# The experts of a mixture layer in three phases of 768 tokens with Strassen products of 384 columns, in place of two phases of 1152 with 288

## The chip, the core and the metric

One core of one Trainium2 chip runs the whole program. The metric is the time of one execution on the device, in microseconds (us), as the median of several runs. The core has five engines that work side by side, each with its own queue that it works off in order: TensorE (PE in the rows) for matmuls, VectorE (DVE), ScalarE (ACT) and GpSimd (POOL) for elementwise work, SyncE (SP) for issuing transfers. Engines wait for each other by semaphores.

## What is computed

```python
N, D, E, F = (2304, 512, 8, 1024)

def _moe2_ref(x, w_gate, w1, w2):
    logits = x @ w_gate
    logits = logits - logits.max()
    P = np.exp(logits)
    for _ in range(8):
        P /= P.sum(1, keepdims=True) + 1e-09
        P /= P.sum(0, keepdims=True) + 1e-09
        P *= N / E
    out = np.zeros((N, D), dtype=np.float32)
    for e in range(E):
        h = np.maximum(x @ w1[e], 0.0)
        ye = h @ w2[e]
        out += P[:, e:e + 1] * ye
    return out

def reference(attn, moe, moe2):
    a = _attn_ref(**attn)                 # 4 batches, 8 heads, 576 positions, causal with decay
    x = tokens_first(a)                   # (2304, 512)
    x = _moe_ref(x, **moe)                # gated SiLU layer, width 1536
    return _moe2_ref(x, **moe2)           # the experts
```

Every token goes through every expert; the gate only weighs the eight results, after eight rounds of normalising its rows and columns ("balancing" below).

## The kernel before

Attention and the gated layer come first (until about 710 us) and are the same in both kernels, up to their last unit, `moe_unit(3)`, into which the first loads of the experts are merged. What follows is the expert stage.

**Slices.** An expert's hidden width of 1024 is worked off in four slices of 256. The tokens are worked off in phases, since the sum over experts, `acc`, is kept on chip for the tokens of one phase only: two phases of 1152 tokens, so 2 x 8 x 4 = 64 slices. For each slice `wload(i)` fetches a piece of `w1` and of `w2` (512 KB each) and splits every number into a rounded part and a rest, because a product in full precision is made of three matmuls of rounded operands (hi x hi, hi x lo, lo x hi). The sums that Strassen's scheme needs of `w1` (tile `sm`) are made by DVE (L544), the rounded parts by ACT (L550, L554), the rests by POOL (L142: tiles `w1l`, `w2l`).

**Up.** `eup(i, g)` computes relu(x w1) for one slice and for one group `g` of 576 tokens, with seven Strassen products in place of eight, each of 288 token columns and six matmuls (L578, `pa`, 128x288). DVE combines the products (L587: tiles `u`, `c`), ACT takes one copy and the relu (L598, L592: `ah`), DVE the rest of the relu (L593: `al`). The products are written to five PSUM buffers in turn.

**Down.** `edown` multiplies with the slice of `w2`: six matmuls of 512 columns for each tile of 128 tokens (L150, `py`), written to two PSUM buffers in turn; DVE adds them to `acc`, weighed by the balanced gate `lg` (L630; the first expert, unweighed, at L623; ACT scales that sum later, at L626). A slice of 1152 tokens has 84 product matmuls and 54 of 512 columns.

**Operands of x.** The seven token-side operands of the Strassen products, in rounded parts and rests, make up `xf`. `xload(b)` makes them for 576 tokens: it reads x back from memory (`xst`), DVE makes four sums (L508: `xt`), ACT the rounded parts (L512: `xf<-xst`, `xf<-xt`), POOL the rests (L142, the same names). There is one buffer for each group, so those of the second phase are made at the turn of the phases, around 1474 to 1518 us.

**Balancing.** After the first slice `gate()` and `balance()` make `lg`: eight rounds, each of nine small DVE instructions (L665 to L679) with one small matmul in the middle of it (L674, `pz`, which sums over partitions). Each round needs the one before it.

**Order.** The order in which each engine works off these instructions is set at build time: a scheduler plays the program through and gives each engine's queue its order; the code's order is only its starting point. The queues then run as they are.

## Time and profile before

| | |
|---|---|
| time, median of 3 runs | 2275.65 us (2272.15 to 2277.56) |
| profiled execution, its own time | 2276.13 us |
| its span, first to last instruction | 2274.3 us |
| PE busy | 2224.4 us, 98% of the span |
| DVE busy | 1688.4 us, 74% |
| POOL busy | 884.6 us, 39% |
| ACT busy | 849.7 us, 37% |
| mean granted clock of TensorE | 0.995 of full speed |

The span is 1.8 us shorter than the time of that same execution. A row of the profile names the line of the code, the engine, the operation, the tile written and the tiles read. Matmuls overlap in PE's pipeline, so that the duration of one (0.3 us) is longer than the distance between two starts; the distance is what a matmul costs.

### The profile page before, as it was taken

Reading aid. Unit: us, or ns where it says so; the run is one execution under the profiler, and the core shown is the slowest. Engines: PE = TensorE matmul, PEld = TensorE weight load, DVE = VectorE, ACT = ScalarE, POOL = GpSimd, SP = SyncE. Lnnn points to the kernel's source line nnn. Section 1 sums busy time; section 2 is a strip of 40 time slices with the busy share of each in tenths; the row PEclk is TensorE's granted clock in tenths of the full one; section 3 lists DMA queues with packets and bytes.
Section 4 is the critical chain, followed back from the end, with each engine's and each line's share of the span. In section 5 each row is a group of like instructions: output and inputs, shape, how many; then the busy total and the mean of one; then the engine's idle time right before and its main releaser. Section 6 shows DMA issues by size and latency. Waiting matters only on the chain.

```text
span 2274.3 us, 36164 instructions
## 1 busy us (share of the span) xinstructions
PE 2224.4 (98%) x13881; PEld 2019.3 (89%) x13881; DVE 1688.4 (74%) x3385; ACT 849.7 (37%) x1936; POOL 884.6 (39%) x668
## 2 busy tenths in 40 slices
PE   7899999999999999999999999989999999999999
PEld 5698899999999898988988989979889898898897
DVE  6678854544535798888878888886888787887876
ACT  7766754454322433322323222333232232322321
POOL 6869863342423432323323233353233232332320
PEclk9999999999999999999999999999999999999999
DMA  8666664454644211111111111121111111111101
GB/s 246 196 213 217 214 229 159 163 171 148 232 160 153 70 46 40 47 47 38 56 38 47 47 39 56 48 90 51 43 43 51 38 56 38 47 47 38 56 29 51
DMA packets 95469, 215.97 MB, mean 95 GB/s; under 512 B 10000, under 2 KB 52288, under 8 KB 83264
## 3 DMA queue, kind: packets, MB, share of 16 engines
q1 hardware_dynamic: 95296, 213.66, 29.1%
q8 instruction: 109, 1.79, 0.3%
q14 instruction: 64, 0.52, 0.1%
HBM read 185.02 MB, written 28.61 MB: 94 GB/s over the span
## 4 chain that ended last, share of the span: by engine, by line
PE 85%; DVE 6%; DMA 4%; ACT 2%; issue 1%; POOL 1%; SPq 0%; DVEq 0%; ACTq 0%; POOLq 0%
PE py L150 39%; PE pa L578 29%; PE pm L150 11%; DMA st<-wf 2%; PE ps_o L340 2%; PE ps_t L309 1%; DVE al L593 1%; DMA xst<-xd 1%; PE ps_s L272 1%; PE ps_s L268 1%; DVE np L274 1%; DVE xt L508 1%; PE ps_o L332 1%; DVE c L587 0%; DMA qk<-qkT 0%
## 5 line engine op out<-in xcount | busy, mean ns | idle before, releaser
L578 PE MATMUL pa<-xf,w1h 128*128 128x288 f32 x3584 | 749.2, 295 | 7.0 <-DVE c L587 6.6
L578 PEld LDWEIGHTS pa<-xf,w1h 128*128 128x128 f32 x3584 | 597.7, 188 | 45.9 <-DVE c L587 8.4
L630 DVE SCALAR_TENSOR_TENSOR acc<-py,lg,acc 128x512 f32<-128x512 f32 x531 | 395.1, 744 | 241.2 <-PE py L150 240.9
L578 PE MATMUL pa<-xf,w1l 128*128 128x288 f32 x1792 | 527.4, 295 | 0.0
L142 POOL TENSOR_TENSOR w2l<-w,w2h 128x1024 fp32r<-128x1024 f32 x64 | 154.8, 2420 | 825.2 <-ACT w2h L554 825.0
L150 PE MATMUL py<-w2h,ah 128*128 128x512 f32 x1152 | 454.1, 394 | 4.2 <-DVE acc L623 2.5
L150 PE MATMUL py<-w2l,ah 128*128 128x512 f32 x1152 | 454.1, 394 | 0.0
L150 PE MATMUL py<-w2h,al 128*128 128x512 f32 x1152 | 453.2, 393 | 0.0
L593 DVE SCALAR_TENSOR_TENSOR al<-c,ah 128x288 fp32r<-128x288 f32 x512 | 426.7, 860 | 7.4 <-ACT ah L592 6.7
L592 ACT ACTIVATE ah<-c 128x288 fp32r<-128x288 f32 x512 | 208.1, 443 | 590.9 <-PE py L150 318.9
L578 PEld LDWEIGHTS pa<-xf,w1l 128*128 128x128 f32 x1792 | 337.0, 188 | 10.5
L150 PE MATMUL pm<-xh,w 128*128 128x288 f32 x1536 | 326.5, 298 | 3.4 <-DVE xa L431 1.9
L150 PEld LDWEIGHTS py<-w2h,al 128*128 128x128 f32 x1152 | 216.3, 188 | 49.9
L150 PEld LDWEIGHTS pm<-xh,w 128*128 128x128 f32 x1536 | 252.0, 188 | 6.2 <-DVE xa L431 2.5
L150 PEld LDWEIGHTS py<-w2h,ah 128*128 128x128 f32 x1152 | 216.4, 188 | 33.3 <-DVE acc L623 2.9
L150 PEld LDWEIGHTS py<-w2l,ah 128*128 128x128 f32 x1152 | 216.3, 188 | 26.0
L142 POOL TENSOR_TENSOR w1l<-w,w1h 128x256 fp32r<-128x256 f32 x192 | 162.0, 870 | 179.1 <-ACT w1h L550 179.1
L150 PE MATMUL pm<-xl,w 128*128 128x288 f32 x768 | 226.4, 295 | 2.6 <-POOL xl L142 2.6
L598 ACT COPY m<-pa 128x288 f32<-128x288 f32 x128 | 50.2, 392 | 436.0 <-PE pa L578 433.6
L150 PE MATMUL py<-ah,w 128*128 128x288 f32 x768 | 174.6, 299 | 3.5 <-DVE xa L431 1.6
L142 POOL TENSOR_TENSOR al<-th,ah 128x288 fp32r<-128x288 f32 x96 | 82.0, 854 | 201.8 <-ACT ah L415 201.8
L142 POOL TENSOR_TENSOR w1l<-sm,w1h 128x1024 fp32r<-128x1024 f32 x64 | 154.6, 2415 | 2.5 <-ACT w1h L550 2.5
(138 smaller groups left out, 3102.6 us busy)
## 6 DMA issues: line engine op xcount, KB each, us to landing
w<-w SPq DMA_DIRECT2D x128, 512.0 KB, 3.6
w<-wsplit SPq DMA_DIRECT2D x54, 1024.0 KB, 5.8
qk<-qkT SPq DMA_DIRECT2D x64, 288.0 KB, 5.5
st<-wf SPq DMA_DIRECT2D x18, 1024.0 KB, 8.4
wsplit<-w SPq DMA_DIRECT2D x18, 1024.0 KB, 5.0
cb<-cumd SPq DMA_DIRECT2D x31, 288.0 KB, 3.3
xd<-xa SPq DMA_DIRECT2D x4, 1152.0 KB
xst<-xd SPq DMA_DIRECT2D x8, 576.0 KB, 6.1
```

The lines of the kernel that those rows point to most:

```text
L142: (eng or nc.gpsimd).tensor_tensor(out=out, in0=src, in1=hi.bitcast(F32), op=ALU.subtract)
L150: nc.tensor.matmul(out=ps, lhsT=a, rhs=b, start=(i == 0), stop=(i == n - 1))
L268: nc.tensor.matmul(out=ps[:, 0:w], lhsT=a[:, qs:qs + P], rhs=kh[:, c0:c0 + w], start=True, stop=False)
L272: nc.tensor.matmul(out=ps[:, 0:w], lhsT=a[:, qs:qs + P], rhs=kl[:, c0:c0 + w], start=False, stop=True)
L274: nc.vector.tensor_tensor_reduce(out=pt[r0:P, c0:c0 + use], in0=ps[r0:P, 0:use], in1=cb[r0:P, c0:c0 + use], scale=-SCALE, scalar=prev, op0 ...
L309: nc.tensor.transpose(pv[:, j, :], pt[r0:P, k0:k0 + P], ident[r0:P, r0:P])
L340: nc.tensor.matmul(out=po[:, c0:w], lhsT=vs[:, j, e].rearrange("p a d -> p (a d)"), rhs=pts[rng][part][:, j, c0:w], start=(i == 0), stop=( ...
L578: nc.tensor.matmul(out=ps, lhsT=w[:, MW[m - 1], k], rhs=x[:, m - 1, hl, k], start=(n == 0), stop=(n == len(ops) - 1))
L592: nc.scalar.activation(out=ah[:, f, tk], in_=src, func=AF.Relu)
L593: nc.vector.scalar_tensor_tensor(out=al[:, f, tk], in0=src, scalar=0.0, in1=ah[:, f, tk].bitcast(F32), op0=ALU.max, op1=ALU.subtract)
L598: nc.scalar.copy(out=m1, in_=p1)
L630: nc.vector.scalar_tensor_tensor(out=a, in0=py, scalar=lg[:, t, e:e + 1], in1=a, op0=ALU.mult, op1=ALU.add)
```

## The change

The experts run in three phases of 768 tokens, so 96 slices; a phase has one group, and its products have 384 columns (768 / 2). A slice has 42 product matmuls of 384 columns and 36 of 512. In all there are 4032 product matmuls in place of 5376, with the same number of columns (1,548,288), and 3456 of 512 columns as before. `wload` runs 96 times in place of 64. `edown(i - 1)` stands whole behind `eup(i)`, where before a part of `edown(i)` stood in its own slice. The operands `xf` are kept in halves of the features, in three buffers that are used in turn, where a phase needs two; their `xload`s stand three and one slices ahead of a phase's last. Some of their rests are made by DVE in place of POOL (for the second half of the later phases, the three operands that are not sums). Line numbers behind L587 are greater by one in the changed kernel.

```diff
@@ -483,40 +483,43 @@
     def pool2(name, bufs, **kw):
         return pool(name, bufs, reuse_waits="tile", **kw)
 
-    xfp = ctx.enter_context(pool2("xfp", 1, side="right"))
+    HT = 384
+    GT = 2 * HT
+    NPH = NT // GT
+    TP = GT // P
+    xfp = ctx.enter_context(pool2("xfp", 3, side="right"))
     wst = ctx.enter_context(pool2("wst", 1, side="right"))
     wsp0 = ctx.enter_context(pool2("wsp0", 1, side="right"))
     xst = ctx.enter_context(pool2("xst", 1, side="right"))
     xf = {}
 
-    def xload(b):
-
-        def part(k):
-            if b not in xf:
-                xf[b] = xfp.tile([P, NF, 2, 2, HB], F32R, tag=f"xf{b % NB}", name="xf")
-            st = xst.tile([P, 2, S], F32, tag="x", name="xst", bufs=2)
-            src = xd[b].rearrange("p (i k) n -> p i k n", i=2)[:, :, k, :]
-            if b < NB:
-                with tc.issue_after(last_dma[0].ins):
-                    last_dma[0] = nc.sync.dma_start(out=st, in_=src)
-            else:
-                nc.sync.dma_start(out=st, in_=src)
-            (b11, b12), (b21, b22) = ((st[:, i, 0:HB], st[:, i, HB:S]) for i in range(2))
-            t = xst.tile([P, 4, HB], F32, tag="t", name="xt")
-            t4, t1, t2, t3 = (t[:, i] for i in range(4))
-            for o, x, y in ((t1, b12, b11), (t3, b22, b12), (t2, b22, t1), (t4, t2, b21)):
-                nc.vector.tensor_tensor(out=o, in0=x, in1=y, op=ALU.subtract)
-
-            for f, src in ((slice(0, 2), st[:, :, 0:HB]), (slice(2, 3), st[:, 1:2, HB:S]), (slice(3, 7), t)):
-                hi, lo = xf[b][:, f, 0, k], xf[b][:, f, 1, k]
-                nc.scalar.copy(out=hi, in_=src)
-                rest(lo, src, hi)
-        return [(1.0, lambda k=k: part(k)) for k in range(2)]
-
-    NPH = 2
-    NB = B // NPH
-    TP = NTILE // NPH
-    merge(moe_unit(3), xload(0) + xload(1))
+    def xload(g, k):
+
+        x = xfp.tile([P, NF, 2, HT], F32R, tag="xf", name="xf")
+        xf[g, k] = x
+        st = xst.tile([P, 2, GT], F32, tag="x", name="xst", bufs=2)
+        t0 = g * GT
+        while t0 < (g + 1) * GT:
+            b, c = divmod(t0, S)
+            n = min(S - c, (g + 1) * GT - t0)
+            src = xd[b].rearrange("p (i k) n -> p i k n", i=2)[:, :, k, c:c + n]
+            with tc.issue_after(last_dma[0].ins) if g == 0 else ExitStack():
+                d = nc.sync.dma_start(out=st[:, :, t0 - g * GT:t0 - g * GT + n], in_=src)
+            if g == 0:
+                last_dma[0] = d
+            t0 += n
+        (b11, b12), (b21, b22) = ((st[:, i, 0:HT], st[:, i, HT:GT]) for i in range(2))
+        t = xst.tile([P, 4, HT], F32, tag="t", name="xt")
+        t4, t1, t2, t3 = (t[:, i] for i in range(4))
+        for o, p, q in ((t1, b12, b11), (t3, b22, b12), (t2, b22, t1), (t4, t2, b21)):
+            nc.vector.tensor_tensor(out=o, in0=p, in1=q, op=ALU.subtract)
+
+        for f, src in ((slice(0, 2), st[:, :, 0:HT]), (slice(2, 3), st[:, 1:2, HT:GT]), (slice(3, 7), t)):
+            hi, lo = x[:, f, 0], x[:, f, 1]
+            nc.scalar.copy(out=hi, in_=src)
+            rest(lo, src, hi, nc.vector if g and k and f.start < 3 else None)
+
+    merge(moe_unit(3), [(1.0, lambda k=k: xload(0, k)) for k in range(2)])
     m_ctx.close()
     hp_ = ctx.enter_context(pool2("hp", 2))
     wsp1 = ctx.enter_context(pool2("wsp1", 1))
@@ -563,24 +566,22 @@
     A11, A12, A22, S1, S2, S3, S4 = range(NF)
     MW = (A11, A12, S4, A22, S1, S2, S3)
 
-    def eup(i, g):
+    def eup(i):
         ph = slices[i][0]
         wh, wl = wts[i][0]
-        x = xf[ph * NB + g]
-        if g == 0:
-            hs[i] = [hp_.tile([P, 2, NB * S], F32R, tag=t, name=t) for t in ("ah", "al")]
-        ah, al = hs[i]
+        x = [xf[ph, k] for k in range(2)]
+        ah, al = hs[i] = [hp_.tile([P, 2, GT], F32R, tag=t, name=t) for t in ("ah", "al")]
 
         def prod(m):
-            ps = ps_a.tile([P, 512], F32, tag="a", name="pa")[:, 0:HB]
+            ps = ps_a.tile([P, 512], F32, tag="a", name="pa")[:, 0:HT]
             ops = [(w, hl, k) for k in range(2) for w, hl in ((wh, 0), (wh, 1), (wl, 0))]
             for n, (w, hl, k) in enumerate(ops):
                 nc.tensor.matmul(
-                    out=ps, lhsT=w[:, MW[m - 1], k], rhs=x[:, m - 1, hl, k], start=(n == 0), stop=(n == len(ops) - 1))
+                    out=ps, lhsT=w[:, MW[m - 1], k], rhs=x[k][:, m - 1, hl], start=(n == 0), stop=(n == len(ops) - 1))
             return ps
 
         def tmp_(tag):
-            return hp_.tile([P, HB], F32, tag=tag, name=tag)
+            return hp_.tile([P, HT], F32, tag=tag, name=tag)
 
         def comb(tag, in0, in1, op=ALU.add):
             t = tmp_(tag)
@@ -588,7 +589,7 @@
             return t
 
         def relu(f, j, src):
-            tk = slice(g * S + j * HB, g * S + (j + 1) * HB)
+            tk = slice(j * HT, (j + 1) * HT)
             nc.scalar.activation(out=ah[:, f, tk], in_=src, func=AF.Relu)
             nc.vector.scalar_tensor_tensor(
                 out=al[:, f, tk], in0=src, scalar=0.0, in1=ah[:, f, tk].bitcast(F32), op0=ALU.max, op1=ALU.subtract)
@@ -680,21 +681,19 @@
                 out=lg, in0=lg, in1=rc.unsqueeze(1).to_broadcast([P, NTILE, E]), op=ALU.mult)
 
     wload(0)
-    split = S // P
+    per = len(slices) // NPH
     for i in range(len(slices)):
+        ph, at = divmod(i, per)
         wload(i + 1)
-        for g in range(NB):
-            eup(i, g)
-            if i + 1 == len(slices) // NPH:
-                merge(xload(NB + g))
-            if g == 0 and i:
-                edown(i - 1, range(split, TP))
-            if g == 1:
-                edown(i, range(0, split))
+        eup(i)
+        if ph + 1 < NPH and at in (per - 3, per - 1):
+            xload(ph + 1, int(at == per - 1))
+        if i:
+            edown(i - 1, range(TP))
         if i == 0:
             gate()
             balance()
-    edown(len(slices) - 1, range(split, TP))
+    edown(len(slices) - 1, range(TP))
 
 
 def kernel(**inputs):
```

Three places in the order of the engines' queues are shown here. In these rows `pz` is the small matmul of a balancing round, `cs`, `rs`, `rc` and `lg` are its tiles on DVE, `pa` and `py` are the products of up and down.

PE, around the seventh of the eight balancing matmuls, before:

```order
L578 MATMUL pa<-xf,w1h 128x288
L150 MATMUL py<-w2h,ah 128x512
L150 MATMUL py<-w2l,ah 128x512
L150 MATMUL py<-w2h,al 128x512
...
L578 MATMUL pa<-xf,w1h 128x288
L578 MATMUL pa<-xf,w1l 128x288
L674 MATMUL pz<-cs,ones 128x8
L578 MATMUL pa<-xf,w1h 128x288 x2
L578 MATMUL pa<-xf,w1l 128x288
L150 MATMUL py<-w2h,ah 128x512
```

PE, the fourth to eighth of these matmuls, in the changed kernel:

```order
L675 MATMUL pz<-cs,ones 128x8
L579 MATMUL pa<-xf,w1h 128x384 x2
L579 MATMUL pa<-xf,w1l 128x384
L579 MATMUL pa<-xf,w1h 128x384 x2
L579 MATMUL pa<-xf,w1l 128x384
L579 MATMUL pa<-xf,w1h 128x384 x2
L579 MATMUL pa<-xf,w1l 128x384
L579 MATMUL pa<-xf,w1h 128x384 x2
L579 MATMUL pa<-xf,w1l 128x384
L675 MATMUL pz<-cs,ones 128x8 x4
L150 MATMUL py<-w2h,ah 128x512
```

Before, products and down matmuls stand between any two balancing matmuls; in the changed kernel twelve product matmuls stand between the fourth and the fifth, and none between the fifth and the eighth. Ahead of the fourth there are six down and thirty product matmuls back to the third.

DVE, the last balancing round and what follows, before:

```order
L671 TENSOR_REDUCE cs<-lg 128x8
L593 SCALAR_TENSOR_TENSOR al<-c,ah 128x288
L587 TENSOR_TENSOR u_10599<-pa,m_10590 128x288
L587 TENSOR_TENSOR u_10608<-pa,u_10599 128x288
...
L676 TENSOR_SCALAR rc<-pz 128x8
L593 SCALAR_TENSOR_TENSOR al<-c,ah 128x288
L677 RECIPROCAL rc<-rc 128x8
...
L678 TENSOR_SCALAR rc<-rc 128x8
L587 TENSOR_TENSOR c<-pa,u_10514 128x288
L679 TENSOR_TENSOR lg<-lg,rc 128x144
```

DVE, the same round in the changed kernel:

```order
L666 TENSOR_REDUCE rs<-lg 128x18
L667 TENSOR_SCALAR rs<-rs 128x18
L668 RECIPROCAL rs<-rs 128x18
L669 TENSOR_TENSOR lg<-lg,rs 128x144
L672 TENSOR_REDUCE cs<-lg 128x8
L677 TENSOR_SCALAR rc<-pz 128x8
L678 RECIPROCAL rc<-rc 128x8
L679 TENSOR_SCALAR rc<-rc 128x8
L680 TENSOR_TENSOR lg<-lg,rc 128x144
L631 SCALAR_TENSOR_TENSOR acc<-py,lg,acc 128x512 x6
```

Before, work on products stands between the instructions of a round; in the changed kernel the last rounds stand alone (four `sm` instructions in the fifth, nothing in the sixth to eighth), and the weighed sums follow right behind them.

POOL, at the turn of the phases, before:

```order
L142 TENSOR_TENSOR xf<-xst,xf 128x2x288
L142 TENSOR_TENSOR xf<-xst,xf 128x288
L142 TENSOR_TENSOR w2l<-w_16522,w2h 128x1024
L142 TENSOR_TENSOR xf<-xt,xf 128x4x288
...
L142 TENSOR_TENSOR w1l<-sm,w1h 128x1024
L142 TENSOR_TENSOR xf<-xt,xf 128x4x288 x2
L142 TENSOR_TENSOR w2l<-w_16765,w2h 128x1024
```

POOL, at the first turn in the changed kernel:

```order
L142 TENSOR_TENSOR w2l<-w_13431,w2h 128x1024
L142 TENSOR_TENSOR xf<-xt,xf 128x4x384
L142 TENSOR_TENSOR w1l<-w_13897,w1h 128x256 x3
L142 TENSOR_TENSOR w1l<-sm,w1h 128x1024
L142 TENSOR_TENSOR xf<-xst,xf 128x2x384
L142 TENSOR_TENSOR xf<-xst,xf 128x384
L142 TENSOR_TENSOR w2l<-w_13592,w2h 128x1024
L142 TENSOR_TENSOR xf<-xt,xf 128x4x384
L142 TENSOR_TENSOR w1l<-w_14049,w1h 128x256 x3
```

Before, the rests of four halves (twelve instructions) stand at the one turn. In the changed kernel two halves are made at the first turn, with four instructions on POOL; one half is made at the second turn, and one half of the second phase was made at the start of the stage, behind the two of the first phase.

## Rows read from the trace of the kernel before

**Rows 1.** Windows: stretches of the expert stage; span, then busy us (instructions) of each engine.

```profile
core 0: us, PE busy (x) PEld busy (x) DVE busy (x) ACT busy (x) POOL busy (x), PEclk, DMA share, GB/s
757.00:874.00 117.00, 113.46 (x691) 101.80 (x690) 100.00 (x249) 43.46 (x91) 36.15 (x25) 1.00 0.15 47
874.00:1474.00 600.00, 600.00 (x3495) 539.52 (x3495) 491.51 (x889) 172.64 (x384) 186.34 (x128) 1.00 0.14 45
1474.00:1518.00 44.00, 36.82 (x201) 31.07 (x200) 42.22 (x65) 15.76 (x31) 27.64 (x16) 1.00 0.23 72
1518.00:2240.00 722.00, 722.00 (x4222) 650.11 (x4220) 577.32 (x1051) 207.73 (x462) 220.18 (x150) 1.00 0.15 47
```

**Rows 2.** Timeline of PE: start, duration, line, operation; twelve products, six down matmuls, the next product.

```profile
1200.86 0.43 PE L578 MATMUL pa<-xf,w1h 128*128 128x288 f32 x2
...
1202.46 0.39 PE L150 MATMUL py<-w2h,ah 128*128 128x512 f32 x1
...
1203.85 0.43 PE L578 MATMUL pa<-xf,w1h 128*128 128x288 f32 x2
```

**Rows 3.** Timeline of PE and ACT, around the balancing; in brackets idle time before, and its releaser.

```profile
855.71 0.50 PE L150 MATMUL py<-w2h,ah 128*128 128x512 f32 x1 [2.47 <-DVE acc L623]
...
865.04 0.28 PE L674 MATMUL pz<-cs,ones 128*128 128x8 f32 x2
...
869.81 5.62 ACT L626 ACTIVATE acc<-acc,lg 128x512 f32<-128x512 f32 x9
```

**Rows 4.** Timeline of DVE: the nine instructions of one balancing round.

```profile
860.27 0.16 DVE L676 TENSOR_SCALAR rc<-pz 128x8 f32<-128x8 f32 x1
860.46 0.20 DVE L677 RECIPROCAL rc<-rc 128x8 f32<-128x8 f32 x1
...
861.27 0.16 DVE L678 TENSOR_SCALAR rc<-rc 128x8 f32<-128x8 f32 x1
861.46 0.31 DVE L679 TENSOR_TENSOR lg<-lg,rc 128x144 f32<-128x144 f32 x1
...
862.06 0.30 DVE L665 TENSOR_REDUCE rs<-lg 128x18 f32<-128x144 f32 x1
862.39 0.18 DVE L666 TENSOR_SCALAR rs<-rs 128x18 f32<-128x18 f32 x1
...
862.84 0.26 DVE L667 RECIPROCAL rs<-rs 128x18 f32<-128x18 f32 x1
863.13 0.31 DVE L668 TENSOR_TENSOR lg<-lg,rs 128x144 f32<-128x144 f32 x1
...
864.09 0.45 DVE L671 TENSOR_REDUCE cs<-lg 128x8 f32<-128x144 f32 x1
```

**Rows 5.** Groups by line and shape, whole run: busy us, mean ns of one | idle before.

```profile
L593 DVE SCALAR_TENSOR_TENSOR al<-c,ah 128x288 fp32r<-128x288 f32 x512 | 426.7, 860 | 7.4 <-ACT ah L592 6.7
L630 DVE SCALAR_TENSOR_TENSOR acc<-py,lg,acc 128x512 f32<-128x512 f32 x531 | 395.1, 744 | 241.2 <-PE py L150 240.9
...
L587 DVE TENSOR_TENSOR c<-pa,u 128x288 f32<-128x288 f32 x256 | 114.4, 447 | 1.9 <-PE pa L578 1.4
...
L142 POOL TENSOR_TENSOR xf<-xt,xf 128x1152 fp32r<-128x1152 f32 x8 | 21.6, 2705 | 9.4 <-ACT xf L512 9.4
```

**Rows 6.** Windows in attention: a stretch with PE partly idle, and the one behind it.

```profile
234.00:240.00 6.00, 3.92 (x22) 2.46 (x20) 5.91 (x15) 3.50 (x10) 2.84 (x3) 1.00 1.01 313
240.50:243.80 3.30, 3.30 (x15) 3.10 (x16) 3.24 (x6) 2.60 (x5) 3.22 (x4) 0.50 0.02 5
```

**Rows 7.** Timeline of POOL, DVE and PE at the turn of the phases.

```profile
1506.09 2.69 POOL L142 TENSOR_TENSOR xf<-xt,xf 128x1152 fp32r<-128x1152 f32 x1 [4.94 <-ACT xf L512]
1508.73 2.55 POOL L142 TENSOR_TENSOR w2l<-w,w2h 128x1024 fp32r<-128x1024 f32 x1
...
1506.38 5.21 DVE L593 SCALAR_TENSOR_TENSOR al<-c,ah 128x288 fp32r<-128x288 f32 x2 [0.25 <-ACT ah L592]
...
1512.02 0.53 PE L578 MATMUL pa<-xf,w1h 128*128 128x288 f32 x2 [3.18 <-DVE c L587]
```

**Rows 8.** Timeline of ACT in the last unit of the gated layer.

```profile
709.77 0.41 ACT L412 ACTIVATE th<-pm 128x288 f32<-128x288 f32 x1 [3.26 <-POOL al L142]
```

## Prediction

> **What bounds the kernel now.** I read the page first: PE is busy for 98% of the span, so only two things can move the time: how long PE's own work takes, and where PE stands still. The windows of the expert stage show the second [rows 1]. For 600 us after 874, and for 722 us after 1518, PE has no idle time at all, while DVE is busy for 82% and POOL for 31%. PE is idle for 3.54 us in the stretch of the first slices and the balancing (757 to 874), and for 7.18 us at the turn of the phases (1474 to 1518). So inside the slices PE is the bound, and DVE is the engine that ends its waits around them. The rest of the program (about 750 us before this stage, and the tail) is the same code.
>
> **Products: fewer and longer.** What a matmul costs is the distance between starts [rows 2]: twelve products of 288 columns from 1200.86 to 1202.46 are 1.60 / 12 = 133.3 ns each, six of 512 from there to 1203.85 are 1.39 / 6 = 231.7 ns. No row shows 384 columns. On the straight line between the two it is 133.3 + 96 x 98.4 / 224 = 175.5 ns. Before, 5376 x 133.3 ns = 716.8 us; after, 4032 x 175.5 ns = 707.5 us: **-9.3 us**. The bounds: a price in proportion to the 288 columns (177.8 ns) gives no gain, one in proportion to the 512 columns (173.8 ns) gives 700.6 us, or -16.2. I take the line, since both ends lie on it. The 3456 down matmuls stay as they are.
>
> The Trainium skill ("TensorE: Matmul & The Clock Gate", section "Back-to-back issue gap") gives for the isolated gap from one matmul to the next N / 2.4 + 2.5 ns, so a fixed part of 2.5 ns for each matmul. By that rule 1344 matmuls less would save only 3.4 us, and the sum below would be 5.9 us higher, about 2291. The trace does not agree: it has 133.3 ns at 288 columns, where the rule gives 122.5.
>
> **Balancing: the work between its rounds is gone.** In a round, DVE works off nine instructions, the last of them `cs`; PE sums over partitions (`pz`), and DVE goes on. The nine take 2.33 us in all [rows 4], with gaps of about 0.03 us some 2.6. `cs` ends at 864.54 [rows 4] and `pz` starts at 865.04 [rows 3]: 0.5 us, and a little more until DVE has its result, say 0.6. A round that stands alone so takes 3.2 us (2.9 to 3.6). Before, PE had products and down matmuls between any two `pz`. In the changed order `pz` four to eight have only twelve products between the first two of them, and PE works in order: it stands at each `pz` until DVE is there. Step by step:
> - fourth `pz`: the 36 matmuls ahead of it take 30 x 0.1755 + 6 x 0.2317 = 6.7 us; DVE has nine instructions of a round (2.6), one `acc` (0.74), four `al` (0.45 to 0.86 each, by the rows of `c` and `al`) and four combinations (some 0.5 each) [rows 5], with PE's 0.6 together 7.7 to 9.4. PE waits about 2 us (1 to 3).
> - fifth: a round of 3.2 and four `sm` instructions (I put them at 0.35 each, an estimate from the row of `c` by their 256 columns), less the twelve products' 2.1: 2.5 us (2 to 3).
> - sixth to eighth: 3 x 3.2 = 9.6 us (8.7 to 10.8).
> - the down matmuls behind the eighth need a free PSUM buffer, so a weighed `acc`, and so the last four instructions of the round (0.95 with gaps [rows 4]), one scaling on ACT (5.62 / 9 = 0.62 [rows 3]) and one `acc` (0.74 [rows 5]): 2.4 us (1.9 to 3).
>
> That is 16.5 us with PE idle. After a stretch in which PE was busy for 3.92 of 6 us the granted clock was 0.50, the lower of its two levels, for 3.3 us [rows 6]. PE stands still for longer here; I add half of such a stretch, 1.65 us (0 to 3.4). Of what stood in this window before, 3.54 us [rows 1] fall away, among them the wait of 2.47 us for the first `acc` [rows 3]. In sum 18.2 - 3.5 = **+14.7 us** (10 to 20). Whatever stands behind these waits on PE is late by them, since the products could have run: PE loses the time for good, as it is the bound of all that follows.
>
> **Turns of the phases: two in place of one.** At the turn before, POOL made a rest of `xt` for 2.69 us and one of `w2l` for 2.55 us without a pause; in the same time DVE stood in two `al` for 5.21 us, and PE waited 3.18 us for the combination behind them [rows 7]. Such waits come to 7.2 us at one turn [rows 1]. In the changed kernel POOL has four `xf` instructions at the first turn and one at the second, in place of twelve, always with weight work between them, and half of a phase's operands is made ahead. But some rests go to DVE, which is the engine that is late there, and 384 columns make each longer by a third. I take 7 us for the first turn (between 2, and one and a half times the old one, 11) and 2 for the second (1 to 3): 9 against 7.2, **+2 us** (-4 to +7).
>
> **Start of the stage.** Three halves in place of four are made behind the last unit of the gated layer, but the loads for the third stand in SP's queue among the weights, and POOL's rests stand between the `al` of that unit. Before, ACT waited there up to 3.26 us for POOL [rows 8] with PE kept busy by other products. One rest more in that place is 2.7 us [rows 5]; I put down about half: **+1.5 us** (0 to +5).
>
> **More weight work: nothing.** `wload` runs 32 times more, so 32 MB more of loads, at a DMA share of 0.15 [rows 1]. POOL has 186.34 / 600 x 23.6 us (84 x 0.133 + 54 x 0.232, the PE time of a slice) = 7.3 us of it for each slice; a slice now takes 42 x 0.1755 + 36 x 0.2317 = 15.7 us, so POOL goes from 31% to 47%. This hurts through DVE: `al` takes 860 ns where a `c` of the same size takes 447 [rows 5], so some 0.41 us of each is waiting for POOL. At half as much POOL work again that is 0.62 us, but there are four `al` in 15.7 us and not eight in 23.6: 16% of DVE's time against 14%. DVE goes from 82% to about 84% and still has a reserve, and five PSUM buffers of products (5 x 6 x 0.1755 = 5.3 us of PE work) cover one wait of 2.5 us. The cost is 0, as long as it does not come twice in a row.
>
> **The sum.** -9.3 + 14.7 + 2 + 1.5 = +8.9 us on the profiled execution's 2276.13: 2285.0 us. That execution lies 0.5 us above the median of 2275.65, which I leave aside.
>
> **Rivals.**
> 1. *Faster: the long product is cheaper than the line.* If a product of 384 columns came to less than 172.1 ns, 13.5 us below the line in sum, the result would be 0.2% (4.55 us, about what a measurement here can tell) below before. At 170 ns the products are 685.4 us, -31.4, and the time 2263. For it: PE's weight loads are busy for 90% of the steady stretch (539.52 of 600), so that a short product may pay for its weights. Against it: from 288 to 512 columns the price of a column falls only from 0.463 to 0.453 ns [rows 2], and 170 ns would be 0.443, less than at 512. Chance 0.12.
> 2. *No difference: the turns lose their waits.* If POOL's rests, spread out as they now are, never stand two in a row with `al` queued behind them, both turns cost about 1 us each, -5 in place of +2; with the balancing at its lower end (+10) and nothing at the start the sum is -9.3 + 10 - 5 = -4, or up to +4 with the balancing as forecast: 2272 to 2280. For it: the order with weight work between. Against it: the weight rests block `al` too. Chance 0.20.
> 3. *Much slower: DVE becomes the bound within slices.* With POOL at 47%, a `w1l`, a `w2l` and an `al` meet more often, and only two PSUM buffers (2 x 1.39 us) stand behind `acc`. If each slice lost 0.3 us, 96 slices lose 29 us: 2314. For it: the 860 ns of `al`. Against it: the 1322 us of steady stretches without a single wait of PE. Chance 0.12.
>
> The forecast itself has 0.56. Its own range is 2280 to 2292.
>
> **The numbers.** Faster by over 0.2% is rival 1 with a little of rival 2: 0.13. Within 0.2%: most of rival 2 and the lower edge of the forecast, 0.21. Slower: the rest, 0.66. The range of 8 in 10 reaches from 2273 (the middle of rival 2; below it lies rival 1) to 2298 (balancing at 20, turns at +7 and the start at +3 give 2297; above it lies rival 3).
>
> **What would show it.** Right, if PE's steady distance is 175 to 176 ns at 384 columns; if the timeline of PE has four waits of about 3 us each for `cs` at its last `pz`, and some 16 us idle in that window; if the steady stretches have no idle PE time; and if the two turns together lose about 9 us. Wrong, if the distance is under 172 ns, if the rounds pass faster than 2.9 us, if slices lose time regularly to `acc` or `c`, or if the turns lose under 3 or over 15 us.

## The result: 0.8% slower, and the profile after

| | before | changed |
|---|---|---|
| median of 6 runs each | 2275.94 us | 2294.35 us (2292.03 to 2299.7) |
| ratio to before, 95% interval | | 1.0080 (1.0067 to 1.0092) |
| span of the profiled run | 2274.3 us | 2291.5 us |

The change costs about 18 us (15 to 21 by the interval), where 9 were forecast. The page of the changed kernel, first lines:

```profile
span 2291.5 us, 33589 instructions
...
PE 2224.6 (97%) x12537; PEld 2018.8 (88%) x12537; DVE 1603.0 (70%) x3157; ACT 921.7 (40%) x1927; POOL 1097.6 (48%) x818
```

Windows of the changed kernel: the start of the expert stage, the balancing, a steady stretch, and the two turns of the phases (they answer to [rows 1]):

```profile
core 0: us, PE busy (x) PEld busy (x) DVE busy (x) ACT busy (x) POOL busy (x), PEclk, DMA share, GB/s
615.00:800.00 185.00, 176.56 (x1178) 169.89 (x1178) 94.87 (x180) 60.29 (x123) 78.57 (x61) 0.98 0.40 137
800.00:880.00 80.00, 66.40 (x321) 58.67 (x320) 63.34 (x155) 23.52 (x45) 28.22 (x20) 0.91 0.16 53
880.00:1230.00 350.00, 350.00 (x1740) 315.61 (x1739) 260.69 (x471) 117.06 (x223) 158.16 (x110) 1.00 0.20 67
...
1230.00:1300.00 70.00, 63.48 (x304) 54.80 (x303) 61.60 (x91) 24.38 (x44) 39.12 (x24) 0.98 0.27 87
1740.00:1800.00 60.00, 58.52 (x290) 52.22 (x289) 48.60 (x80) 23.84 (x43) 32.33 (x21) 1.00 0.25 77
```

The same windows of the kernel before, for the two first:

```profile
615.00:800.00 185.00, 183.39 (x1289) 175.41 (x1288) 101.48 (x219) 60.05 (x131) 69.94 (x57) 1.00 0.38 133
800.00:880.00 80.00, 76.94 (x476) 70.18 (x475) 73.81 (x178) 29.71 (x62) 26.48 (x19) 1.00 0.15 47
```

PE's idle time at the start grows from 1.6 to 8.4 us, in the balancing from 3.1 to 13.6, and the clock is below full speed in both (0.98 and 0.91). In the steady stretch PE has no idle time, as before, and DVE is busy for 74% (260.69 of 350) where it was 82%.

To have idle time and lost clock in one number, I took every matmul's distance to the next start from the first product on, less the steady distance of its kind in the same run, and added up what is over, stretch by stretch:

| lost over the steady distances, us | before | changed | difference | forecast |
|---|---|---|---|---|
| start, from the first product to 800 | 4.3 | 13.9 | +9.7 | +1.5 |
| balancing, 800 to 880 | 4.4 | 17.7 | +13.3 | +14.7 |
| turns of the phases | 8.9 | 11.3 | +2.3 | +2 |
| the matmuls themselves, by slices | | | -8.2 | -9.3 |
| sum | | | +17.1 | +8.9 |

From the first product to the end the profiled runs take 1655.9 and 1675.4 us, +19.5; 2.4 us of it lie scattered outside these four. (The program ahead of the first product, the same in both, happened to be 2.3 us shorter in the profiled run of the changed kernel.)

**Matmuls.** Timeline of PE: the first product of a slice, twelve products and six down matmuls in a row, and the first product 24 slices later:

```profile
1322.29 0.51 PE L579 MATMUL pa<-xf,w1h 128*128 128x384 f32 x2
...
1344.24 0.52 PE L579 MATMUL pa<-xf,w1h 128*128 128x384 f32 x2
...
1346.36 0.39 PE L150 MATMUL py<-w2h,ah 128*128 128x512 f32 x1
...
1347.76 0.34 PE L579 MATMUL pa<-xf,w1h 128*128 128x384 f32 x1
...
1698.54 0.51 PE L579 MATMUL pa<-xf,w1h 128*128 128x384 f32 x2
```

A slice takes (1698.54 - 1322.29) / 24 = 15.68 us (forecast 15.7). Counted in the same way a slice before takes 23.64, and 96 x 15.68 - 64 x 23.64 is -8 us. The twelve products here take 2.12 / 12 = 177 ns each; over all steady distances between products the mean is 176.0 ns, and 132.7 before.

**Balancing.** Timeline of PE, the last five balancing matmuls and the matmuls behind them, and of DVE, one round:

```profile
844.34 0.39 PE L675 MATMUL pz<-cs,ones 128*128 128x8 f32 x2 [0.93 <-DVE cs L672]
...
848.96 0.39 PE L675 MATMUL pz<-cs,ones 128*128 128x8 f32 x2 [1.80 <-DVE cs L672]
852.03 0.59 PE L675 MATMUL pz<-cs,ones 128*128 128x8 f32 x2 [2.68 <-DVE cs L672]
855.31 0.60 PE L675 MATMUL pz<-cs,ones 128*128 128x8 f32 x2 [2.68 <-DVE cs L672]
858.58 0.59 PE L675 MATMUL pz<-cs,ones 128*128 128x8 f32 x2 [2.68 <-DVE cs L672]
861.77 0.79 PE L150 MATMUL py<-w2h,ah 128*128 128x512 f32 x1 [2.59 <-DVE acc L631]
862.36 0.63 PE L150 MATMUL py<-w2l,ah 128*128 128x512 f32 x1
...
865.71 0.39 PE L150 MATMUL py<-w2h,ah 128*128 128x512 f32 x1
...
855.94 0.17 DVE L677 TENSOR_SCALAR rc<-pz 128x8 f32<-128x8 f32 x1 [0.69 <-PE pz L675]
...
858.12 0.41 DVE L672 TENSOR_REDUCE cs<-lg 128x8 f32<-128x144 f32 x1
859.22 0.17 DVE L677 TENSOR_SCALAR rc<-pz 128x8 f32<-128x8 f32 x1 [0.69 <-PE pz L675]
```

A bare round, one with no other work between its instructions, takes 3.28 us (852.03 to 855.31 to 858.58), and PE stands for it. What follows starts at the lower clock. Windows of the changed kernel:

```profile
846.00:862.00 16.00, 3.57 (x16) 2.88 (x15) 11.67 (x43) 1.80 (x3) 0.00 (x0) 0.69 0.00 1
862.00:864.00 2.00, 2.00 (x5) 1.58 (x6) 0.37 (x1) 1.99 (x4) 0.00 (x0) 0.50 0.00 0
864.00:866.00 2.00, 2.00 (x7) 1.56 (x6) 0.75 (x1) 0.00 (x0) 0.00 (x0) 0.60 0.00 0
866.00:870.00 4.00, 4.00 (x19) 3.24 (x18) 2.03 (x3) 0.77 (x2) 0.00 (x0) 1.00 0.00 0
```

Nine matmuls, from 861.77 to the start of the next at 865.71, take 3.94 us, where nine steady distances of 0.230 us are 2.07: about 1.9 us lost (forecast 1.65).

**Start.** Timeline of DVE, POOL, ACT and PE, in two places:

```profile
616.11 2.66 DVE L515 TENSOR_TENSOR xt<-xst 128x384 f32<-128x384 f32 x2 [0.49 <-DMA xst<-xd]
...
616.17 3.47 POOL L142 TENSOR_TENSOR xf<-xst,xf 128x768 fp32r<-128x768 f32 x2 [1.53 <-ACT xf L519]
...
621.79 1.47 ACT L519 CAST xf<-xt 128x1536 fp32r<-128x1536 f32 x1 [3.73 <-DVE xt L515]
...
623.31 1.65 PE L579 MATMUL pa<-xf,w1h 128*128 128x384 f32 x4 [2.15 <-ACT xf L519]
...
743.64 1.02 ACT L553 CAST w1h<-w 128x256 fp32r<-128x256 f32 x3 [1.95 <-PE py L150]
...
746.46 0.47 ACT L599 COPY m<-pa 128x384 f32<-128x384 f32 x1
...
746.98 0.61 PE L579 MATMUL pa<-xf,w1h 128*128 128x384 f32 x2 [2.24 <-ACT m L599]
...
748.53 2.41 POOL L142 TENSOR_TENSOR w2l<-w,w2h 128x1024 fp32r<-128x1024 f32 x1
...
749.42 3.63 DVE L594 SCALAR_TENSOR_TENSOR al<-c,ah 128x384 fp32r<-128x384 f32 x2
752.98 2.50 DVE L547 TENSOR_TENSOR sm<-w 128x256 f32<-128x256 f32 x2
...
755.99 0.71 PE L579 MATMUL pa<-xf,w1h 128*128 128x384 f32 x2 [2.27 <-DVE c L588]
```

Three waits of PE of 2.2 us each: for the first operands (DVE's sums and ACT's cast of a larger half, beside POOL), for a copy that stands on ACT behind 2.8 us of weight casts of the next slice, and for a combination behind two `al` and two `sm`, both slow while POOL works on weight rests. In the kernel before none of the three is there. Their sizes are those of one execution: other three-phase runs whose queues have the same order here show the first wait at 2.10 (run 3 below), 3.22 (run 4) and 3.31 us (run 2).

**Turns.** Timeline of POOL, DVE and PE at the first turn, and of PE at the second (as [rows 7]):

```profile
1260.69 3.42 POOL L142 TENSOR_TENSOR xf<-xst,xf 128x768 fp32r<-128x768 f32 x2
...
1258.56 4.70 DVE L515 TENSOR_TENSOR xt<-xst 128x384 f32<-128x384 f32 x2
...
1265.24 0.80 PE L150 MATMUL py<-w2h,ah 128*128 128x512 f32 x1 [2.64 <-DVE acc L631]
...
1775.42 0.61 PE L579 MATMUL pa<-xf,w1h 128*128 128x384 f32 x2 [1.49 <-DVE c L588]
```

At the first turn it is the pattern of before, with `xt` and `acc` in the place of `al` and `c`.

### The profile page after: what moved, and what is told of

Read it like the earlier page. It is cut to its first block, busy times and chain, and to the rows that moved or that the text cites. A ratio compares the mean times of both kernels' runs of the same rounds, so it can differ in the third digit from the quotient of the medians.

```text
span 2291.5 us, 33589 instructions
## 1 busy us (share of the span) xinstructions
PE 2224.6 (97%) x12537; PEld 2018.8 (88%) x12537; DVE 1603.0 (70%) x3157; ACT 921.7 (40%) x1927; POOL 1097.6 (48%) x818
## 4 chain that ended last, share of the span: by engine, by line
PE 84%; DVE 7%; DMA 4%; ACT 1%; issue 1%; POOL 1%; SPq 0%; POOLq 0%; ACTq 0%; DVEq 0%
PE py L150 39%; PE pa L579 30%; PE pm L150 11%; DMA st<-wf 2%; PE ps_o L340 1%; PE ps_t L309 1%; DVE al L594 1%; DVE xt L515 1%; PE ps_s L272 1%; PE ps_s L268 1%; DVE np L274 1%; DVE st L117 1%; DMA xst<-xd 1%; DMA qk<-qkT 1%; DVE acc L631 0%
## 5 line engine op out<-in xcount | busy, mean ns | idle before, releaser
L579 PE MATMUL pa<-xf,w1h 128*128 128x384 f32 x2688 | 694.8, 339 | 10.2 <-DVE c L588 5.0
L142 POOL TENSOR_TENSOR w2l<-w,w2h 128x1024 fp32r<-128x1024 f32 x96 | 232.0, 2416 | 700.9 <-ACT w2h L557 700.9
L579 PEld LDWEIGHTS pa<-xf,w1h 128*128 128x128 f32 x2688 | 494.1, 188 | 52.2 <-DVE c L588 6.7
L593 ACT ACTIVATE ah<-c 128x384 fp32r<-128x384 f32 x384 | 188.3, 522 | 793.8 <-issue 385.1
L579 PE MATMUL pa<-xf,w1l 128*128 128x384 f32 x1344 | 454.3, 338 | 0.0
L594 DVE SCALAR_TENSOR_TENSOR al<-c,ah 128x384 fp32r<-128x384 f32 x384 | 281.6, 771 | 10.0 <-ACT ah L593 9.7
L142 POOL TENSOR_TENSOR w1l<-w,w1h 128x256 fp32r<-128x256 f32 x288 | 230.8, 828 | 114.5 <-ACT w1h L553 113.6
L579 PEld LDWEIGHTS pa<-xf,w1l 128*128 128x128 f32 x1344 | 252.6, 188 | 0.7
L142 POOL TENSOR_TENSOR w1l<-sm,w1h 128x1024 fp32r<-128x1024 f32 x96 | 230.5, 2401 | 8.4 <-ACT w1h L553 8.4
L547 DVE TENSOR_TENSOR sm<-w 128x256 f32<-128x256 f32 x192 | 80.2, 457 | 100.5 <-DMA w<-w 99.1
```

The source lines that it names most:

```text
L142: (eng or nc.gpsimd).tensor_tensor(out=out, in0=src, in1=hi.bitcast(F32), op=ALU.subtract)
L547: nc.vector.tensor_tensor(out=sm[:, o], in0=x, in1=y, op=op)
L579: nc.tensor.matmul(out=ps, lhsT=w[:, MW[m - 1], k], rhs=x[k][:, m - 1, hl], start=(n == 0), stop=(n == len(ops) - 1))
L593: nc.scalar.activation(out=ah[:, f, tk], in_=src, func=AF.Relu)
L594: nc.vector.scalar_tensor_tensor(out=al[:, f, tk], in0=src, scalar=0.0, in1=ah[:, f, tk].bitcast(F32), op0=ALU.max, op1=ALU.subtract)
```

## The experiments

The first question was why the rounds stand bare. The gate is first needed by the second expert: the four slices of the first are added without weights. In two phases these are 4 x 23.64 = 95 us of work that needs no gate; in three phases 4 x 15.68 = 63 us. Theory A grew into A2 along the way: this work runs out before the rounds are done. All ratios below are to the kernel before in runs beside it, with their 95% interval; "over" or "under" the changed kernel is by the difference of the ratios to its 1.0080.

**1. The gate brought in early.** `gate` split, its first 1536 tokens beside the gated layer (its definition and buffers move up with it):

```diff
-    merge(moe_unit(3), [(1.0, lambda k=k: xload(0, k)) for k in range(2)])
...
+    merge(moe_unit(3), [(1.0, lambda k=k: xload(0, k)) for k in range(2)] + [(1.0, lambda t=t: gate(t, t + 512)) for t in (0, 512, 1024)])
...
-            gate()
+            gate(1536, NT)
```

> Three phases, with the gate's logits of the first 1536 tokens brought in and transposed beside the last unit of the gated layer, so that only 768 tokens' logits are left for after it. Theory A (the changed kernel loses some 13 us because its last five balancing rounds stand bare, and they stand bare because the balancing starts too late for the unweighed work that is there): with all eight rounds between products the window of the balancing loses under 4 us in place of 17, and the time is 12 to 14 us under the changed kernel, about 2281. Rival B (the unweighed work of a phase of 768 tokens is too short, four slices of 15.7 us, wherever the rounds stand): the idle time only moves to another wait, and the gain is under 4 us. Rival C (the loss is at the start of the stage and stays): under 4 us, or a new loss of some us beside the gated layer.

Measured: 1.0075 (1.0060 to 1.0091), so next to nothing. The loss in the balancing fell from 17.7 to 9.3 us, but the edit had cost something elsewhere: its transposes took a PSUM buffer that products use, no product could start before the gated layer's end, and the start lost more. So the run told little of the theories, and it was made again (5).

The same edit in the kernel before:

> The kernel before with the same edit. Theory A: its rounds are covered already, only the wait of 2.5 us for the first acc can go: 0 to 4 us under the kernel before. If the edit gained as much here as in three phases, it would gain by something else than the cover of the rounds.

Measured: 1.0013 (1.0001 to 1.0024), 3 us over the kernel before and not under it. Its wait in the balancing went (lost there: 0.9 us in place of 4.4), but the start lost its products here too, 9.1 us from 744 to 800.

**2. One round.**

```diff
-        for _ in range(8):
+        for _ in range(1):
```

> Three phases with one balancing round; the other seven are left out, so the weights are not balanced. Theory A: the bare rounds fall away, 12 to 17 us under the changed kernel. Rival C: under 5 us, since the start of the stage and the turns lose what they lost. DVE has 63 small instructions less, some 18 us of its time, which is no gain where PE is the bound.

Measured: 0.9983 (0.9971 to 0.9995), 22 us under the changed kernel, more than expected. Window of the balancing:

```profile
800.00:880.00 80.00, 80.00 (x402) 72.12 (x401) 61.06 (x119) 30.76 (x57) 37.52 (x26) 1.00 0.23 73
```

All of the loss there is gone (0.4 us in place of 17.7), and the start still loses 15.6 us, with a longer wait for the first operands than the changed kernel's 2.15, though its queues have the same order up to there:

```profile
625.09 1.65 PE L579 MATMUL pa<-xf,w1h 128*128 128x384 f32 x4 [3.31 <-ACT xf L519]
```

Rival C is out for the larger part.

**3. The rests of the operands on POOL.**

```diff
-            rest(lo, src, hi, nc.vector if g and k and f.start < 3 else None)
+            rest(lo, src, hi)
```

> Three phases, with all rests of the token operands on POOL again (three instructions on POOL more at each turn, the same fewer on DVE). If at a turn DVE waits for POOL (theory A), the turns lose more: 11 us in sum become 12 to 16, the time 1 to 5 us longer. Rival: DVE is late by its own work; then the turns lose 1 to 4 us less.

Measured: 1.0063 (1.0048 to 1.0078). The turns lose 9.9 us in place of 11.3: not more, as this run's theory A (DVE waits for POOL at a turn) had it, but a little less. The rests that the change moved to DVE bring nothing; that DVE's own work is what is late there is the better reading, though the intervals overlap. This run also shows how far two executions differ: up to the first turn its queues have the same order as the changed kernel's, and yet its start loses about 3 us less. The wait of 2.27 us for the combination is 0.81 us there, and the granted clock in the 3.5 us behind it 1.00 where the changed kernel has 0.56:

```profile
758.53 0.62 PE L579 MATMUL pa<-xf,w1h 128*128 128x384 f32 x2 [0.81 <-DVE c L588]
```

**4. More work without weights.**

```diff
-            if ph == 0 and e == 0:
...
+            if ph == 0 and e < 2:
...
-                if ph == 0 and e == 1 and s == 0:
+                if ph == 0 and e == 2 and s == 0:
```

> Three phases; in the first phase the second expert's slices are added without weights as well, and the sum is scaled one expert later, so that the weights of that expert are left out (eight slices need no gate, in place of four; all matmuls and rounds stay). The order has products between all eight rounds. Theory A2 (the unweighed work, four slices of 15.7 us for 768 tokens against four of 23.6, runs out before the rounds are done): the balancing window loses under 2 us in place of 17, and the time is 13 to 18 us under the changed kernel, or 1.000 to 1.002 of the kernel before. Rival (the rounds cost DVE time that the products need, so 72 small instructions slow the slices wherever they stand): under 6 us.

Measured: 1.0003 (0.9992 to 1.0014), 17.5 us under the changed kernel. Window of the balancing:

```profile
800.00:880.00 80.00, 79.15 (x401) 71.30 (x400) 72.76 (x165) 24.57 (x48) 32.89 (x25) 1.00 0.20 66
```

The second expert's weights are left out of the result, but all rounds and all matmuls are still there; the rounds only have cover. From the first product to the end this run takes 1660.2 us, the one with one round 1656.0, the changed kernel 1675.4. The rival (rounds cost wherever they stand) is out.

**5. The gate early, once more**, with its transposes in a buffer of the gated layer:

```diff
+    merge(moe_unit(3), [(1.0, lambda k=k: xload(0, k)) for k in range(2)] + [(1.0, lambda t=t: gate(t, t + 512, ps_m, "m")) for t in (0, 512, 1024)])
...
+            gate(1536, NT, ps_z, "z")
```

> Three phases with the early gate once more, its transposes now in a buffer of the gated layer, so that the first products can start where they do in the changed kernel. Theory A2: the balancing starts some 10 us earlier, six of the rounds have products between them, and the time is 7 to 12 us under the changed kernel, 2282 to 2287; the start of the stage loses what it lost there (14 us). Rival: the early gate itself disturbs the gated layer, and the start of the stage loses 5 us more, as in the first run with it.

Measured: 1.0056 (1.0043 to 1.0070), 5.5 us under the changed kernel, less than expected. The balancing loses about 6 us less, one bare round being left in place of three. The start loses about 3 us more, with a new wait of 2.03 us beside the gated layer, so that the rival holds in part. Why an earlier gate gains so little in the balancing, the next run shows.

**6. The rests of the second slice's weights on DVE.**

```diff
-            rest(lo[:, o], src, hi[:, o])
+            rest(lo[:, o], src, hi[:, o], nc.vector if i == 1 else None)
...
-        rest(lo2, st2, hi2)
+        rest(lo2, st2, hi2, nc.vector if i == 1 else None)
```

> Three phases, the rests of the second slice's weights made by DVE in place of POOL. Theory D (at the start of the stage DVE's relu rests stand behind POOL's weight rests, PE then waits 2.3 us for a combination and runs at the lower clock level for a few us; and the rests of the last batch, on which the gate waits, stand behind them too): this wait of PE falls away, the gate starts about 7 us earlier, and the time is 4 to 10 us under the changed kernel. Rival (DVE has too much work there itself): no gain, within 2 us.

Measured: 1.0071 (1.0053 to 1.0090), so 2 us or nothing. Theory D was right on its waits: of the three at the start the third is gone, and the start loses 10.0 us in place of 13.9. After run 3, this difference of single executions may be partly chance. But the balancing lost about as much as in the changed kernel. By line, the gate's transposes (L646) and the last step of the rounds (L680), with first and last start in us, in the changed kernel:

```profile
L646 PE MATMUL pz<-ident,ls x18: 208/208/231, 768.6 to 791.8; 16*128 16x16 f32 x18
...
L680 DVE TENSOR_TENSOR lg<-lg,rc x8: 308/309/850, 816.6 to 859.9; 128x144 f32<-128x144 f32 x8
```

and in this run:

```profile
L646 PE MATMUL pz<-ident,ls x18: 207/208/232, 760.1 to 782.3; 16*128 16x16 f32 x18
...
L680 DVE TENSOR_TENSOR lg<-lg,rc x8: 296/307/684, 806.5 to 856.8; 128x144 f32<-128x144 f32 x8
```

The gate starts 8.5 us earlier and the rounds end 3.1 us earlier. As long as there is other work, DVE's queue has it between a round's instructions, and a round takes some 10 us (before: eight `pz` from 795.8 to 865.0); it takes 3.28 when nothing else is left. So an earlier start is mostly used up by slower rounds, and the work runs out all the same.

**7. Two buffers of operands in place of three.**

```diff
-    xfp = ctx.enter_context(pool2("xfp", 3, side="right"))
+    xfp = ctx.enter_context(pool2("xfp", 2, side="right"))
```

> Three phases with two buffers for the token operands in place of three, so that no half of the second phase is made at the start and both are made at the turns. Theory E (the third half is what makes the start lose 14 us in place of 4): the start loses 5 to 8 us less and the turns a few us more, in sum 0 to 6 us faster. Rival (the start is late by its longer operands of 384 columns and by the order of weight work on ACT and POOL): the start gains 0 to 2 us, the turns lose 4 to 15 us more, and the time is 2 to 15 us longer than the changed kernel.

Measured: 1.0115 (1.0098 to 1.0133), 8 us over the changed kernel. The start lost 14.8 us, no less: the third half is not what makes it lose, and made ahead it spares time at the turns (the second turn loses over 6 in place of 1.8). Theory E is out.

**8. A second sum.** The second expert's slices are added without weights to a sum of their own (`acc2`):

```diff
+    acc2 = ep.tile([P, TP, DM], F32, name="acc2")
...
-            if ph == 0 and e == 0:
...
+            if ph == 0 and e < 2:
+                a = (acc, acc2)[e][:, tt, :]
...
-                if ph == 0 and e == 1 and s == 0:
+                if ph == 0 and e == 2 and s == 0:
                     nc.scalar.mul(out=a, in_=a, mul=lg[:, t, 0:1])
+                    nc.vector.scalar_tensor_tensor(
+                        out=a, in0=acc2[:, tt, :], scalar=lg[:, t, 1:2], in1=a, op0=ALU.mult, op1=ALU.add)
```

> Three phases; in the first phase the second expert's slices are added to a sum of their own, without weights, and that sum is weighed and added to the first (six instructions of DVE more) when the third expert begins. The result is the reference's. Theory A2 (the unweighed work runs out before the rounds are done): as in the run that left the second expert's weights out, 1.000 to 1.003 of the kernel before, about 2276 to 2282; the balancing window loses under 4 us. Rival: the six scalings on ACT and twelve weighed instructions on DVE at the third expert stop PE as the bare rounds did; then 1.004 to 1.008.

Measured: 1.0004 (0.9992 to 1.0015), as with the weights left out; the balancing loses 3.0 us. The rival is out.

**9. The second sum, and the start mended**: with it the edits of 3 and 6, and the next slice's weights behind the first copy on ACT:

```diff
-        nc.scalar.copy(out=m1, in_=p1)
+        first.append(nc.scalar.copy(out=m1, in_=p1))
...
-        wload(i + 1)
+        if i:
+            wload(i + 1)
         eup(i)
+        if i == 0:
+            with tc.issue_after(first[0].ins):
+                wload(1)
```

> The three-phase kernel with the second sum, the rests of the second slice's weights on DVE, the weight casts of the second slice held back on ACT behind the first copy of a product, and all rests of the token operands on POOL. Theory D and F (at the start PE waits 2.2 us for that copy, which stands behind 3 us of weight casts on ACT, and 2.3 us for a combination behind POOL's rests): the start loses 4 to 8 us less than in the changed kernel, the turns 0 to 2 less, and the time is 0.994 to 0.999 of the kernel before, faster than both. Rival: the waits at the start only move; then 0.999 to 1.003, as with the second sum alone.

Measured: 0.9986 (0.9974 to 0.9998).

> As the run with the second sum and the start mended, but without holding back the weight casts on ACT. Theory F (the copy behind the casts costs 2 to 3 us): 2 to 3 us slower than with them held back. Rival (PE waits there anyway): within 1 us of it.

Measured: 0.9985 (0.9975 to 0.9996), without holding the weights back. Both end a little under the kernel before, by 3 us; for the first of them that is the upper edge of what was expected, and its interval reaches to the rival's 0.999. Holding back brings no time: the medians are 2275.46 us with it and 2275.01 without, so the 2 to 3 us of theory F aren't there. With it the wait of 2.24 us for the copy does go, and a wait of 0.76 us for a combination comes in its place. The start loses 10.5 us against 9.3 all the same, since PE waited 3.38 us for the first operands against 2.06; but those are the two sizes that this wait also takes with queues in the same order (2.15 in the changed kernel, 3.31 in run 2), so it can't be put down to the edit. Window of the start of the second of them:

```profile
615.00:800.00 185.00, 177.77 (x1200) 170.54 (x1199) 102.48 (x197) 61.86 (x126) 74.74 (x57) 1.00 0.40 137
```

**10. Less work without weights in the kernel before.**

```diff
-            if ph == 0 and e == 0:
+            if ph == 0 and e == 0 and s < 3:
...
-                if ph == 0 and e == 1 and s == 0:
+                if ph == 0 and e == 0 and s == 3:
```

> The kernel before (two phases, 288 columns), with only three slices of the first expert added without weights in place of four; the sum is scaled, and the weights used, one slice earlier. The result is the reference's, no work is added, and only the unweighed work is shorter: 71 us in place of 95, where the changed kernel has 63. Theory A2: the last rounds stand bare here too, the balancing window loses 10 to 17 us in place of 4, and the time is 6 to 13 us over the kernel before. Rival (the bare rounds come from the new shape of the phases, 384 columns or the order of edown): no change, within 3 us.

Measured: 1.0025 (1.0014 to 1.0036), 5.7 us over the kernel before. Window of the balancing, and PE's waits at its end:

```profile
800.00:880.00 80.00, 73.21 (x425) 65.58 (x424) 65.34 (x159) 28.26 (x58) 26.71 (x19) 0.96 0.15 47
```

```profile
854.91 0.39 PE L674 MATMUL pz<-cs,ones 128*128 128x8 f32 x2 [2.68 <-DVE cs L671]
857.88 0.80 PE L150 MATMUL py<-w2h,ah 128*128 128x512 f32 x1 [2.58 <-DVE acc L630]
```

A bare round, with the wait of 2.68 us of the changed kernel, appears in two phases with 288 columns, with nothing changed but the slice from which weights are used. The balancing loses 10.8 us against 4.4. So neither the columns nor the shape of a phase are needed to make rounds bare: less work ahead of the gate's first use is enough. With 95, 71 and 63 us of such work the balancing loses 4.4, 10.8 and 17.7 us. Of the size in time, 6 to 13 us, barely the lower edge came.

## Why the prediction was right, and where it was off

The time, 2294.35 us, lies in the range (2273 to 2298) and on the side forecast, outside the forecast's own range of 2280 to 2292. The change cost 17 us in the profiled executions, where 9 were forecast. Nearly all of the miss is the start of the stage; that the range held is luck in so far as its room was meant for the balancing and the turns, and these came out near the middle of theirs.

**The balancing** was the main term and held: forecast +14.7, measured +13.3; a bare round 3.28 us against 3.2, the lower clock 1.9 against 1.65. The fourth and the fifth `pz` waited less than put down (0.93 and 1.80 us, where 2 and 2.5 were), and the window had lost 4.4 us before where 3.54 were taken. Of the signs, four waits of about 3 us came as three of 2.68 and one of 1.80, and 16 us idle as 13.6. The order of the queues gave the place, and the rows of before gave the price. What the prediction didn't see is the cause, which runs 4, 8 and 10 show: the work without weights shrinks with the phase.

**The products.** The sum was near (-8.2 against -9.3), its parts were not. The step that put 384 columns on the line between the rows of 288 and 512 gave 175.5 ns, and steady distances are 176.0; with 132.7 in place of 133.3 ns for 288 columns the products alone give 4032 x 176.0 - 5376 x 132.7 ns = -4 us. The 133.3 came from twelve products in rows of two decimals, which leave it open by up to 0.8 ns, or 4 us over 5376 products. The other 4 us come from the down matmuls, put at no change: their mean steady distance went from 231.6 to 230.4 ns, x 3456. It goes with the buffers: in both kernels the distance alternates from slice to slice, 232.7 and 230.2 ns before, 233.3 and 227.5 in the changed kernel, as the two buffers of weights, `ah` and `al` do. What it is about the buffers is open. So the -8.2 near the forecast's -9.3 is in part luck. For the products alone the rule of the Trainium skill ("TensorE: Matmul & The Clock Gate", section "Back-to-back issue gap"), -3.4 us, came nearer than the line, though its distance for one matmul (162.5 ns at 384 columns) is 13 ns too short: at 288 columns it is 10 ns too short, and in the sum the two cancel.

**The start of the stage** is the step that failed: +1.5 with a bound of +5, measured +9.7. It counted one more rest on POOL beside the gated layer (PE does wait 1.1 us there, at 707.5, but for a `th` that stands on DVE behind the four sums `xt` of a half) and priced nothing of what the change makes longer: the first operands, with a third more columns, and the order of casts and rests of the next slice's weights around the first products. Run 7 shows that the third half, which the step was about, isn't the cause; run 6 and the two runs of 9 that the wait behind POOL's rests is a part of it: their starts lose 9.3 to 10.5 us, those of the six comparable traces with these rests on POOL about 10.7 to 15.7, the changed kernel's 13.9 among them. Even the least of these is 6 us above the 4.3 of before, past the bound of +5. How much each of the other two waits costs is not shown: the first differs by over 1 us between executions, and without the second the time stayed.

**The turns** were +2 and came out at +2.3 (9.5 and 1.8 us where 7 and 2 were put down, against 8.9 before where 7.2 were). **Weight work at nothing** held: no wait in the steady stretches, and rival 3 is out. The working behind it did not: it had DVE at 84% and a longer `al`, and DVE fell to 74%, with a shorter mean of `al` than before though each is a third wider ([rows 5] has 860 ns):

```profile
L594 DVE SCALAR_TENSOR_TENSOR al<-c,ah 128x384 fp32r<-128x384 f32 x384 | 281.6, 771 | 10.0 <-ACT ah L593 9.7
```

Rivals 1 and 2 did not come: the product distance is above 172.1 ns, and the turns kept their waits.

## What to carry to other kernels

When the work of a phase is cut, count what else was hidden behind it: a chain of small instructions that a first phase covers needs a certain time of independent work, and a shorter phase may no longer have it. Then more independent work ahead of the chain's first use (a second sum here, 17 us) helps, and starting the chain earlier much less (8.5 us of start gave 3.1 at the end), as a covered chain is slowed by what covers it. And a stage's start deserves its own list of waits, with each operand's new size. Before a single wait is put down to an edit, look at what it takes in another execution with the same order of queues: the wait for the first operands was 2.1 to 3.3 us here with nothing changed.

## What the runs showed of the hardware that was not expected

The mean of `al` on DVE fell from 860 ns at 288 columns to 771 at 384, with POOL busy for 45% of the steady stretch (158.16 of 350) in place of 31%. Wider rows are not faster: an `al` that meets no work of POOL takes 448 ns at 288 columns and 550 at 384. What fell is the time of those that overlap with POOL, from 1107 to 978 ns, and their share, from 320 of 512 to 198 of 384. So the mean cost of `al` beside POOL doesn't follow POOL's share; where the two meet in the order of the queues counts for more, which is a reading of these two kernels and was not tested by itself.

The distance of the 512-column matmuls, with nothing of their shape changed, alternates from slice to slice with the buffers that they use, and its mean fell by 1.2 ns.

The same order of queues doesn't give the same waits in each execution: the four sums `xt` ahead of the first operands took 5.7 us on DVE in the changed kernel (616.11 to 621.76) and 6.8 in run 2 (616.73 to 623.53), with POOL at work beside them, and PE's wait behind them went from 2.15 to 3.31 us.
